# Block-recurrent attention and SwiGLU on one core: pair 5's own weights beside the next batch's scores, small steps on ScalarE, squares summed ahead of the matmul, orders redealt

## The chip, the cores and the metric

The kernel runs on 1 core of one Trainium2 chip. The metric is the time of one execution on the device, in microseconds (us). Times are medians of several executions; the profile is of one further execution, which has its own time. A core has TensorE (PE; its weight loads are shown apart as PEld), VectorE (DVE), ScalarE (ACT), GpSimd (POOL) and SyncE (SP). Each works through its own instructions in the order given; transfers are put on queues, here by SP and by ScalarE.

## The reference

```python
# x (8, 8, 512, 64): batch, head, token, depth; state (8, 8, 32, 64)
scores = scale * np.matmul(x, state.transpose(0, 1, 3, 2))      # scale = 1/8
a = np.exp(scores - scores.max(-1, keepdims=True))
a /= a.sum(-1, keepdims=True) + 1e-09
xread = np.matmul(a, state)                                     # tokens read the states
scores2 = scale * np.matmul(state, x.transpose(0, 1, 3, 2))
a2 = np.exp(scores2 - scores2.max(-1, keepdims=True))
a2 /= a2.sum(-1, keepdims=True) + 1e-09
sread = np.matmul(a2, x)                                        # states read the tokens
x = np.concatenate([xread, sread], axis=2)                      # 544 rows a batch
x = x.transpose(0, 2, 1, 3).reshape(4352, 512)                  # heads side by side
rms = np.sqrt(np.mean(x * x, axis=-1, keepdims=True) + 1e-06)
xn = x / rms * rms_g
g = xn @ w_gate                                                 # 512 -> 1536
silu = g * (1.0 / (1.0 + np.exp(-g)))
return silu * (xn @ w_val) @ w_out                              # 1536 -> 512
```

Everything is float32 to the kernel's matmuls.

## The kernel before

**Tiling.** There are 8 batches of 512 token rows, and at the end the 256 state rows of all batches together. A token's row is its attention weights times the states, so the kernel doesn't form it for the hidden layer: for each batch it multiplies the states with `w_gate` and `w_val` first (the batch's *own weights*), and multiplies the attention weights `aT_s`, already scaled by the norm, with these. The own weights come in six pairs of blocks of 128 hidden columns, pair 0 to pair 5 (`mp`).

**The stages of a batch.** In batches 1 to 7 the hidden layer (`hidden_seven`) takes for each pair seven block products instead of eight (L849; sums of blocks are made beforehand), ScalarE copies them out of PSUM (three copies a pair, L901 among them, and the Silu, L903), VectorE finishes them (L912, L925). The projection (`project_twice`) uses the seven-product scheme at two levels (L1153), with copies by ScalarE (L1166), sums by VectorE and combining steps by GpSimd (`combine`, L1181 and the lines behind it). Batch 0 is computed plainly (L745, L952). The states' rows go through `state_norm`, `hidden_seven` and `project_seven` (L1015).

**The attention of the next batch** runs within the hidden layer and the projection of the present one, in small pieces:

- `scores`: a transpose of the packed state, its copy out of PSUM (L321, `stT`), four VectorE transposes of `x_b` in blocks of 32 (L339), a store of the result to DRAM (`x_d`, L341) and four loads of it in another layout (`xG`, L346), all five on ScalarE's queue; then 8 matmuls of float32 (16 records in the trace) for the scores (L356).
- `tokens_read`: the softmax (exponentials at L428, one for each half `e`), `stT_g`, the states times the norm's weights (L431), the reads (L449), their squares (L456), the row sums (`rms_on_blocks`, with `ss` at L404), the power -0.5 on GpSimd (L300), its spreading along the rows by TensorE (`along_rows`, L307) and the product with `aT_s`.
- `states_read`: a softmax the other way (exponential at L607), the read products (L643), the division by the sum (`sr`, L654), a transpose, and its copy out of PSUM into `xsT` (L660).
- `own_weights`: 8 matmuls (16 records, L702), two copies by ScalarE (L714), four sums by GpSimd (`more_of_v`, L729 and behind). Pairs 0 and 1 are made ahead of their batch, with the projection of the batch before; pairs 2 to 5 within the batch's hidden layer.

The matmuls of the scores, the own weights and the state reads use a part of the PE array each (tiles of 64x32, 128x32; the profile shows the tile's size as 64\*32), and eight or more of them in a row are called a *group* below, as the profile's timeline shows them in one line. Consecutive groups of such tiles, with no 128x128 matmul between, are called a stretch.

**PSUM.** Five pools: `aps` (2 buffers, name `at`), `vps` (2, `pv`), `fx` (2), `fy` and `fz` (1 each, `f`). The scores, the attention's transposes and sums and the own weights of pairs 1, 3 and 5 are in `aps`; those of pairs 0, 2 and 4 in `vps`.

**The order of everything is written out by hand.** Each part of the work is a Python generator, a *stream*; strings of letters say which stream takes its next step: `ORDER` up to batch 0, `FIRST` for batch 1, `PERIOD` for each of batches 2 to 6, `LAST` for batch 7, `STATES` for the end. Every engine's instructions, and the transfers on SP's and ScalarE's queues, come in the order that results. The letters of `PERIOD`:

| letter | stream |
|---|---|
| h, t, u | hidden layer: products (TensorE), copies (ScalarE), sums (VectorE) |
| p, c, k, o | projection: products, copies, sums, stores of the output (SP's queue) |
| v, x | own weights of pairs 2 to 5: products, copies |
| w | `slot_sums`, then the products of pairs 0 and 1 of the next batch |
| a, s | `tokens_read` and `states_read` of the next batch |
| l, f, g | loads of `x` and the state of the batch after next, of the weights, of the quarters' sums, on SP's queue |

In `LAST` the letter a stands for `state_norm` and the sums of the first pair of the states' weights (`sums_of_w`, L806 to L812); in `STATES` y stands for those of the other pairs.

Of the kernel before, what the change touches and what calls it, by code (L numbers as in the profile page):

```python
# [8 lines left out]
F32 = mybir.dt.float32  # L9
# [5 lines left out]
ALU = mybir.AluOpType  # L15
ACTF = mybir.ActivationFunctionType
# [3 lines left out]
P = 128  # L20
# [11 lines left out]
)  # L32

PERIOD = (
    "vlhhatthhtaxxhvuxuthhthuhtauuhhtuhuhuthtahtuaaahuhhtuhuhuxhxtutxhthukkkhtaakavfx"
    "xxvgahuhuthuuuxhthhuuxtahtaaaaahuaxhuthhtuhhthhthhsppusuuuuffutaauuhpsspuppppukp"
    "ukkkkckkaakkgppkkcpppakooskakakakkppppacpppappppcckpfppcakakapppaakkkasskkgkaagg"
    "pppppppppppaakakkooakgapssskaaakkkoosspppcfpaawwsslpssxxxpcoowxxxfg"
)

FIRST = (
    "vqahtaqaahhathhthhqxhuuuxthaqatvquvxthxqxqhtquhuuhhhutqhfqttuaaqxhhhtquqqaaxuhxh"
    "uxhtuthhtvuuhkqktxqhkxukuGhtuaaaahuathhahxtuhGtauhhuuhhutstufhhtusahuuatfuhhpuuu"
    "aphtuuppuplkpfuakkpkppkpkkpppspskcckgkkappkGppkppocapkaggpaakpsokakpppagckpapakk"
    "kskpscakakppkpagkaapagcaappkgaskpkppappkkspsppaposaakkskppppaawcswsxoofsxlpoxwxs"
    "cofxox"
)
LAST = (
    "vxhhffththhtuhhhavuttuuhhtfuhhgxxthhhuuuxxtuthuhtthuhuxhutuvxxxvhthhutkxghhtuhut"
    "kxxhuukhtuhthhthhhhhuuuuttuthhhuuuuhtuhuutuupphuukkppcpapkkkkkpppppppppppkkkpcpp"  # L50
    "ckkppkckpkkpkpckkkpppkkkpkoppkpppagcpppppfkpkkkkkkkkppaaaapkpggppppacpcggooooooo"
    "a"
)
STATES = (
    "hththtyyhuhuhhttuhhhyyytyuhutuhhhutthtuyyhhuuyhhthhhuyututyyyhhtyuhhthuuuhhuhtth"
    "ythuuuyyyutuhuhuytuuyhthhuuhthtuhuhutuuppkhpuucppkkccpkpkpc"
)


# [1 line left out]
def kernel(  # L61
# [23 lines left out]
    B, H, S, D = x.shape  # L85
    Ns = state.shape[2]
# [44 lines left out]
    def load_x(b, *queues):  # L131
# [6 lines left out]
        for c in range(NC):  # L138
# [10 lines left out]

    GE.tensor_tensor(out=consts.tile([P, NC], F32, name="first_pow"), in1=mhalf,  # L150
                     in0=ones.to_broadcast([P, NC]), op=ALU.pow)
    bounds = consts.tile([P, 3], F32, name="bounds")
    for i, bound in enumerate((-896.0 - 7.5 / 16, 1.0, 255.0 * 128)):
        GE.memset(bounds[:, i:i + 1], bound)
    rms_g = consts.tile([P, NI], F32, name="rms_g")

# [156 lines left out]
    def scores(b, packed, soft):  # L313

        xb = x_sb[b]
        stT = one.tile([P, 4, Ns], F32, name="stT")
        tp = aps.tile([P, 4, Ns], F32, name="at")
        TE.transpose(out=tp.rearrange("p j n -> p (j n)"),
                     in_=packed.rearrange("p e d -> p (e d)"), identity=ident)
        yield  # L320
        VE.tensor_copy(stT, tp)  # L321
        yield "step"

        if b < 2:
            xT = one.tile([P, 4, NC, P], F32, name="xT", tag="xT")
            for c in range(NC):
                tp = aps.tile([P, 4, P], F32, name="at")
                for j in range(4):
                    TE.transpose(out=tp[:, j, :], in_=xb[:, c, P * j:P * j + P], identity=ident)  # L329
                yield  # L330
                SE.copy(xT[:, :, c, :], tp)
                yield "step"
            xT = xT.rearrange("p j c t -> p j (c t)")
        else:


            xB = one.tile([P, 4, 4, NC, Ns], F32, name="xB", tag="xT")
            for q in range(4):
                VE.transpose(out=xB[:, q], in_=xb[:, q // 2::2, :, Ns * (q % 2):Ns * (q % 2) + Ns])  # L339
                yield  # L340
            nc.scalar.dma_start(out=x_d[b % 2].rearrange("q g f r -> (g f) q r"),  # L341
                                in_=xB.rearrange("p q j c t -> p q (j c t)"))
            yield
            xT = one.tile([P, 4, 4, P], F32, name="xG", tag="xT")
            for q in range(4):
                nc.scalar.dma_start(  # L346
                    out=xT[Ns * q:Ns * q + Ns].rearrange("f g j r -> f g (j r)"),
                    in_=x_d[b % 2][q].rearrange("g f r -> f g r"))
                yield
            xT = xT.rearrange("p g j r -> p j g r")  # L350


        sp = [aps.tile([P, S], F32, name="at") for e in range(2)]
        for j in range(4):
            for e in range(2):
                TE.matmul(out=sp[e][Ns * j:Ns * j + Ns, :], lhsT=stT[D * e:D * e + D, j, :],  # L356
                          rhs=xT[D * e:D * e + D, j],
                          start=True, stop=True)
        yield


        sS = read[b] = one.tile([P, 2, NC, P], F32, name="sS")
        eS = one.tile([P, 2, S // Ns, Ns], F32, name="eS", tag="eS")
        soft.update(st=stT, e=eS, raw=[eS[:, e] for e in range(2)])
        for e in range(2):
            VE.transpose(out=eS[:, e].rearrange("p k n -> p (k n)"),
                         in_=(sp[e] if b < 2 else
                              sp[e].rearrange("p (g c t) -> p g t c", g=4, c=NC)))
            yield
            SE.copy(sS[:, e].rearrange("p c t -> p (c t)"), sp[e])  # L370
            yield "step" if e else None
# [17 lines left out]
    def rms_on_blocks(b, sq):  # L389


        n = S // Ns
        VE.transpose(out=sq[:, 1, :], in_=sq[:, 0, :])
        yield
        part = one.tile([P, n], F32, name="part")
        VE.reduce_sum(out=part, in_=sq[:, 1, :].rearrange("p (k f) -> p k f", f=Ns), axis=AXX)
        yield
        sp = aps.tile([P, n], F32, name="at")
        TE.matmul(out=sp, lhsT=groups.rearrange("p i t -> p (i t)"), rhs=part,
                  start=True, stop=True)  # L400
        yield
        ss = two.tile([P, NC], F32, name="ss")
        for g in range(4):
            VE.tensor_scalar(ss[Ns * g:Ns * g + Ns], sp[Ns * g:Ns * g + Ns, g::4], 1e-6, None,  # L404
                             op0=ALU.add)
        yield "step"
        ri = mean_root(ss, NC)
        yield
        rp = along_rows(ri, NC)
        yield  # L410
        return rp

    def tokens_read(b):
# [9 lines left out]
        for e in range(2):  # L423
# [4 lines left out]
            SE.activation(out=eS[:, e], in_=eS[:, e], func=ACTF.Exp, scale=SCALE)  # L428
            yield "step"
        stT_g[b] = two.tile([P, 4, Ns], F32, name="stT_g")  # L430
        VE.tensor_tensor(out=stT_g[b], in0=stT, in1=rms_g.unsqueeze(2).to_broadcast([P, 4, Ns]),  # L431
                         op=ALU.mult)
        yield
        aT_s[b] = two.tile([P, 2, S], F32, name="aT_s")
        for e in range(2):
# [153 lines left out]
    def states_read(b):  # L589
# [61 lines left out]
        yield  # L651
        sr = two.tile([P, 2 * D], F32, name="sr")
        for e in range(2):
            VE.tensor_scalar(sr[:, D * e:D * e + D], rp[:, e, :], z2[:, e:e + 1], None,  # L654
                             op0=ALU.mult)
        yield
        tp = aps.tile([P, 4, Ns], F32, name="at")
        TE.transpose(out=tp.rearrange("p j n -> p (j n)"), in_=sr, identity=ident)
        yield
        VE.tensor_copy(xsT[:, :, Ns * b:Ns * b + Ns], tp)  # L660
        yield "step"

    def state_norm():

        sq = one.tile([P, NI, NT], F32, name="sqT", tag="eS")
        SE.activation(out=sq, in_=xsT, func=ACTF.Square, scale=DM ** -0.5)
        yield
        sp = aps.tile([P, NT // P], F32, name="at")
        for r in range(NT // P):
            for i in range(NI):  # L670
                TE.matmul(out=sp[:, r:r + 1], lhsT=sq[:, i, P * r:P * r + P], rhs=ones,
                          start=(i == 0), stop=(i == NI - 1))
        yield
        ss = two.tile([P, NT // P], F32, name="sst")
        VE.tensor_scalar(ss, sp, 1e-6, None, op0=ALU.add)
        ri = mean_root(ss, NT // P)
        yield
        rp = along_rows(ri, NT // P)
        yield
        for i in range(NI):  # L680
            VE.scalar_tensor_tensor(out=xsT[:, i, :], in0=xsT[:, i, :], scalar=rms_g[:, i:i + 1],
                                    in1=rp[:, 0:NT], op0=ALU.mult, op1=ALU.mult)
        sums_of_x()
        yield
# [4 lines left out]
    def own_weights(b, mp):  # L689
# [4 lines left out]
        def products():  # L694
            w = w_sb.pop(b * (NM // 2) + mp)
            for e in range(2):
                pv.append(vps.tile([P, 4 * P], F32, name="pv") if b and mp % 2 == 0 else
                          aps.tile([P, 4 * P], F32, name="at") if b or mp else
                          fx.tile([P, 4 * P], F32, name="f"))
            for j in range(4):  # L700
                for e in range(2):
                    TE.matmul(out=pv[e][Ns * j:Ns * j + Ns, :],  # L702
                              lhsT=stT_g[b][D * e:D * e + D, j, :],
                              rhs=w[D * e:D * e + D, j].rearrange("p m k f -> p (m k f)"),
                              start=True, stop=True)
            if b == 0 or b == 1 and mp < 2:
                fetch(b * (NM // 2) + mp + W_BUFS)
            yield
# [686 lines left out]
```

## Time and profile before

| | us |
|---|---|
| median of 3 runs | 752.94 (752.94, 752.58, 754.74) |
| the profiled execution, its own time | 752.98 |
| its span, first to last instruction | 751.2 |

The mean granted clock of TensorE was 0.999 of full speed. Four periods of the order `PERIOD`, each window from one matmul of the hidden layer to the same matmul of the next batch: the columns are the window, and then the busy time and number of instructions of each engine, the granted clock, the DMA share and GB/s.

| window (us) | length | PE | PEld | DVE | ACT | POOL | clock | DMA share | GB/s |
|---|---|---|---|---|---|---|---|---|---|
| 219.35 to 299.51 | 80.16 | 80.16 | 68.21 | 64.96 | 35.14 | 35.10 | 1.00 | 0.56 | 190 |
| 299.51 to 379.86 | 80.35 | 80.35 | 68.38 | 64.63 | 35.13 | 34.80 | 1.00 | 0.58 | 197 |
| 379.86 to 460.53 | 80.67 | 80.67 | 68.38 | 65.11 | 35.13 | 35.65 | 1.00 | 0.58 | 196 |
| 460.53 to 540.69 | 80.16 | 80.16 | 68.22 | 64.53 | 35.14 | 34.77 | 1.00 | 0.58 | 197 |

Lines of a timeline in the next sections begin with the start and the length of a group of like instructions in us, then the engine, the line, the operation, output <- inputs by the program's names, the tile or shape, and how many instructions it groups. As matmuls overlap, a group's length reaches beyond the start of the next. A line of costliest groups has, behind the shapes and the count, the busy time and the mean ns of one instruction.

### The profile page before, as it was taken

What the parts mean: (1) busy time and instruction counts of PE and PEld (TensorE: products, weight loads), DVE (VectorE), ACT (ScalarE), POOL (GpSimd) and SP (SyncE); (2) the same over time, 40 slices, a digit from 0 to 9 for tenths busy, and PEclk for the clock granted to TensorE, in tenths of its full rate; (3) what the DMA queues carried; (4) which work ended last, traced back from release to release, by engine and by line L of the source; (5) the groups of instructions that cost most, each with busy time, mean ns of one, the idle gap of its engine ahead of it and who ended that gap; (6) DMA issues with size and microseconds to landing.
All of it is one profiled execution on the core that took longest, in us unless ns stands there. A gap on an engine that the chain in (4) does not pass through costs nothing.

```text
span 751.2 us, 14331 instructions
## 1 busy us (share of the span) xinstructions
PE 744.2 (99%) x5636; PEld 598.3 (80%) x5636; DVE 589.4 (78%) x1010; ACT 352.9 (47%) x549; POOL 265.8 (35%) x359
## 2 busy tenths in 40 slices
PE   9999999999999999999999999999999999999997
PEld 7734444779977997889887987799788987899996
DVE  4898968799947995799768994799479955888862
ACT  6999961555155434552265325542555336411220
POOL 3100021531293128432654237503831285224600
PEclk9999999999999999999999999999999999999999
DMA  9997934982784276617672578437760856041411
GB/s 295 288 319 251 366 116 179 319 307 108 229 273 140 75 293 219 224 33 298 212 276 57 191 252 285 115 140 257 236 206 28 309 177 252 20 154 65 149 42 29
DMA packets 60995, 146.16 MB, mean 195 GB/s; under 512 B 14848, under 2 KB 31744, under 8 KB 54016
## 3 DMA queue, kind: packets, MB, share of 16 engines
q1 hardware_dynamic: 47808, 125.78, 47.2%
q10 hardware_dynamic: 13120, 19.47, 8.9%
q8 instruction: 45, 0.74, 0.4%
q14 instruction: 22, 0.18, 0.1%
HBM read 116.46 MB, written 28.77 MB: 193 GB/s over the span
## 4 chain that ended last, share of the span: by engine, by line
PE 98%; DVE 1%; issue 0%; POOL 0%; ACT 0%; POOLq 0%
PE f L849 39%; PE f L1153 31%; PE pv L745 6%; PE f L952 6%; PE at L702 3%; PE pv L702 3%; PE f L1015 2%; PE f L1288 2%; PE at L643 1%; PE at L356 1%; PE at L449 1%; PE at L307 0%; PE pv L516 0%; PE at L329 0%; PE at L617 0%; PE at L511 0%
## 5 line engine op out<-in xcount | busy, mean ns | idle before, releaser
L849 PE MATMUL f<-aT_s,v 128*128 128x256 f32 x504 | 119.3, 382 | 0.0
L849 PEld LDWEIGHTS f<-aT_s,v 128*128 128x128 f32 x504 | 94.7, 190 | 23.2 <-issue 9.2
L1181 POOL TENSOR_TENSOR kept<-kept 128x256 f32<-128x256 f32 x28 | 22.7, 811 | 205.8 <-DVE kept L1193 204.6
L1166 ACT COPY kept<-f 128x512 f32<-128x512 f32 (+1 forms) x56 | 29.6, 531 | 136.8 <-PE f L1153 80.1
L849 PE MATMUL f<-aT_t,vs 128*128 128x256 f32 x336 | 87.0, 383 | 0.0
L912 DVE TENSOR_TENSOR g<-g,f 128x512 f32<-128x512 f32 x84 | 57.3, 686 | 36.3 <-PE f L849 25.2
L1153 PE MATMUL f<-w,h 128*128 128x128 f32 x588 | 74.3, 276 | 0.0
L849 PEld LDWEIGHTS f<-aT_t,vs 128*128 128x128 f32 x336 | 62.7, 190 | 14.6 <-POOL vs L729 3.4
L1153 PEld LDWEIGHTS f<-w,h 128*128 128x128 f32 x588 | 69.6, 192 | 4.2 <-issue 4.1
L903 ACT ACTIVATE hb<-g 128x1024 f32<-128x1024 f32 x42 | 44.4, 1057 | 53.3 <-DVE g L912 53.2
L729 POOL TENSOR_TENSOR vs<-v 128x256 f32<-128x256 f32 x42 | 31.4, 747 | 102.9 <-ACT v L714 102.8
L300 POOL TENSOR_TENSOR ri<-ss,mhalf 128x4 f32<-128x4 f32 (+1 forms) x9 | 11.6, 1291 | 100.8 <-DVE ss L381 72.2
L901 ACT COPY g<-f 128x512 f32<-128x512 f32 x42 | 24.6, 585 | 45.2 <-PE f L849 45.2
L745 PE MATMUL pv<-aT_s,v 128*128 128x512 f32 x96 | 44.1, 598 | 0.0
L952 PE MATMUL f<-wo,hb 128*128 128x512 f32 x96 | 43.8, 597 | 0.0
L849 PE MATMUL f<-aT_s,vs 128*128 128x256 f32 x168 | 43.7, 383 | 0.0
L849 PE MATMUL f<-aT_t,v 128*128 128x256 f32 x168 | 43.4, 381 | 0.0
L1153 PE MATMUL f<-wo,hb 128*128 128x128 f32 x336 | 42.3, 275 | 0.0
L1153 PE MATMUL f<-wo,h 128*128 128x128 f32 x336 | 42.2, 275 | 0.0
L925 DVE TENSOR_TENSOR hb<-hb,f 128x512 f32<-128x512 f32 (+1 forms) x48 | 31.0, 646 | 13.3 <-PE f L849 13.3
L1153 PEld LDWEIGHTS f<-wo,hb 128*128 128x128 f32 x336 | 40.4, 192 | 1.2 <-issue 0.8
L925 DVE TENSOR_TENSOR hb<-hb,c 128x512 f32<-128x512 f32 (+1 forms) x48 | 36.2, 754 | 5.9 <-ACT hb L903 5.1
(225 smaller groups left out, 1649.4 us busy)
## 6 DMA issues: line engine op xcount, KB each, us to landing
w_m<-w_d SPq DMA_DIRECT2D x48, 1024.0 KB
w<-t_d SPq DMA_DIRECT2D x49, 576.0 KB
out_dram<-kept SPq DMA_DIRECT2D x28, 256.0 KB
raw<-in_moe_w_val_dram SPq DMA_DIRECT2D x6, 1024.0 KB
raw<-in_moe_w_out_dram SPq DMA_DIRECT2D x6, 1024.0 KB
w_d<-w_m SPq DMA_DIRECT2D x6, 1024.0 KB
x_b<-in_x_dram SPq DMA_DIRECT2D x6, 1024.0 KB
x_d<-xB ACTq DMA_DIRECT2D x6, 1024.0 KB
```

The costliest lines, as they stand in the source:

```text
L702: TE.matmul(out=pv[e][Ns * j:Ns * j + Ns, :], lhsT=stT_g[b][D * e:D * e + D, j, :], rhs=w[D * e:D * e + D, j].rearrange("p m k f -> p (m k ...
L729: GE.tensor_tensor(out=vs[:, 0], in0=a21, in1=a22, op=ALU.add)
L745: TE.matmul(out=to[0], lhsT=lhs(i, k), rhs=r, start=(i == 0), stop=(i == len(rhs) - 1))
L849: TE.matmul(out=ps[:, i, 0:half], lhsT=l[:, i, :], rhs=r, start=(start and i == 0 and k == 0), stop=(k == len(lhs) - 1), skip_group_check= ...
L901: SE.copy(gates(q)[1], q["x"][:, :, 0:half])
L903: SE.activation(out=hb[:, 2 * mp:2 * mp + 2, 0:n].rearrange("p m (c t) -> p m c t", c=2), in_=q["g"][:, :, :, 0:half], func=ACTF.Silu if s ...
L912: VE.tensor_tensor(out=to, in0=to, in1=q[ps][:, :, 0:half], op=ALU.add)
L925: VE.tensor_tensor(out=part, in0=part, in1=val, op=ALU.mult)
L952: TE.matmul(out=banks[r], lhsT=hb[:, m, P * r:P * r + P], rhs=wo[:, m, :], start=(m == 0), stop=(m == NM - 1))
L1153: TE.matmul(out=to[half][:, slot, :], lhsT=lhs[:, k, :], rhs=rhs[:, k, :], start=(fresh and n in (0, 4) and k == 0), stop=(k == QM - 1), s ...
L1166: SE.copy(of_half(k, i), banks[name][i])
L1181: GE.tensor_tensor(out=k[:, 4:8:3], in0=k[:, 5:6].to_broadcast([P, 2, QD]), in1=k[:, 4:8:3], op=ALU.add)
```

## The change

1. The four order strings `PERIOD`, `FIRST`, `LAST` and `STATES` are dealt anew; `ORDER` stays. In `PERIOD` the product step of pair 5's own weights now follows directly on the step of the scores' matmuls; in the string before, the two stood apart. `PERIOD` has 307 letters before and 307 after.
2. Pair 5's own weights go to the PSUM pool `vps` in place of `aps` (which the scores use).
3. For batches 2 to 7, five steps of the attention go from VectorE to ScalarE: the copies to `stT` and `xsT`, the addition of 1e-6 (`ss`, four instructions; its constant in a fourth column of `bounds`), `stT_g` (four instructions instead of one) and `sr` (two).
4. In `state_norm`, GpSimd sums the four blocks of squares with two additions; then 2 matmuls with a column of ones in place of 8.

The strings of `PERIOD`, before and after (the other three are left out):

```diff
-    "vlhhatthhtaxxhvuxuthhthuhtauuhhtuhuhuthtahtuaaahuhhtuhuhuxhxtutxhthukkkhtaakavfx"
-    "xxvgahuhuthuuuxhthhuuxtahtaaaaahuaxhuthhtuhhthhthhsppusuuuuffutaauuhpsspuppppukp"
-    "ukkkkckkaakkgppkkcpppakooskakakakkppppacpppappppcckpfppcakakapppaakkkasskkgkaagg"
-    "pppppppppppaakakkooakgapssskaaakkkoosspppcfpaawwsslpssxxxpcoowxxxfg"
+    "vahhthtxthahhhhxuutxuthahaaathatuuhluhhuhtvtvfxutuxhaxhthaghuaxhhxuauutfuxhhukkk"
+    "tthhhthgauvuhtuhhkthtauhaaxaxtauhhuausufufxhutsththhaugauuthuhuughupaptuhsuuupkg"
+    "kpkkpkkapppkcppkkpkppcgpppkkpkaapopkspaaapkpkkpppasacpkaaccksppkpkkpcaakspkpaaak"
+    "asaappskpksspskppkaakppkgoooppppkaakappppkasoalwfswossxpxfxcwxxxcoo"
```

The rest of the diff:

```diff
...
@@ -149,8 +149,8 @@
 
     GE.tensor_tensor(out=consts.tile([P, NC], F32, name="first_pow"), in1=mhalf,
                      in0=ones.to_broadcast([P, NC]), op=ALU.pow)
-    bounds = consts.tile([P, 3], F32, name="bounds")
-    for i, bound in enumerate((-896.0 - 7.5 / 16, 1.0, 255.0 * 128)):
+    bounds = consts.tile([P, 4], F32, name="bounds")
+    for i, bound in enumerate((-896.0 - 7.5 / 16, 1.0, 255.0 * 128, 1e-6)):
         GE.memset(bounds[:, i:i + 1], bound)
     rms_g = consts.tile([P, NI], F32, name="rms_g")
 
@@ -318,7 +318,7 @@
         TE.transpose(out=tp.rearrange("p j n -> p (j n)"),
                      in_=packed.rearrange("p e d -> p (e d)"), identity=ident)
         yield
-        VE.tensor_copy(stT, tp)
+        (VE.tensor_copy if b < 2 else SE.copy)(stT, tp)
         yield "step"
 
         if b < 2:
@@ -401,8 +401,8 @@
         yield
         ss = two.tile([P, NC], F32, name="ss")
         for g in range(4):
-            VE.tensor_scalar(ss[Ns * g:Ns * g + Ns], sp[Ns * g:Ns * g + Ns, g::4], 1e-6, None,
-                             op0=ALU.add)
+            SE.activation(out=ss[Ns * g:Ns * g + Ns], in_=sp[Ns * g:Ns * g + Ns, g::4],
+                          func=ACTF.Identity, bias=bounds[Ns * g:Ns * g + Ns, 3:4])
         yield "step"
         ri = mean_root(ss, NC)
         yield
@@ -428,8 +428,13 @@
             SE.activation(out=eS[:, e], in_=eS[:, e], func=ACTF.Exp, scale=SCALE)
             yield "step"
         stT_g[b] = two.tile([P, 4, Ns], F32, name="stT_g")
-        VE.tensor_tensor(out=stT_g[b], in0=stT, in1=rms_g.unsqueeze(2).to_broadcast([P, 4, Ns]),
-                         op=ALU.mult)
+        if b < 2:
+            VE.tensor_tensor(out=stT_g[b], in0=stT,
+                             in1=rms_g.unsqueeze(2).to_broadcast([P, 4, Ns]), op=ALU.mult)
+        else:
+            for j in range(4):
+                SE.activation(out=stT_g[b][:, j], in_=stT[:, j], func=ACTF.Copy,
+                              scale=rms_g[:, j:j + 1])
         yield
         aT_s[b] = two.tile([P, 2, S], F32, name="aT_s")
         for e in range(2):
@@ -651,13 +656,16 @@
         yield
         sr = two.tile([P, 2 * D], F32, name="sr")
         for e in range(2):
-            VE.tensor_scalar(sr[:, D * e:D * e + D], rp[:, e, :], z2[:, e:e + 1], None,
-                             op0=ALU.mult)
+            to, z = sr[:, D * e:D * e + D], z2[:, e:e + 1]
+            if b < 2:
+                VE.tensor_scalar(to, rp[:, e, :], z, None, op0=ALU.mult)
+            else:
+                SE.activation(out=to, in_=rp[:, e, :], func=ACTF.Copy, scale=z)
         yield
         tp = aps.tile([P, 4, Ns], F32, name="at")
         TE.transpose(out=tp.rearrange("p j n -> p (j n)"), in_=sr, identity=ident)
         yield
-        VE.tensor_copy(xsT[:, :, Ns * b:Ns * b + Ns], tp)
+        (VE.tensor_copy if b < 2 else SE.copy)(xsT[:, :, Ns * b:Ns * b + Ns], tp)
         yield "step"
 
     def state_norm():
@@ -665,11 +673,13 @@
         sq = one.tile([P, NI, NT], F32, name="sqT", tag="eS")
         SE.activation(out=sq, in_=xsT, func=ACTF.Square, scale=DM ** -0.5)
         yield
+        for n in (2, 1):
+            GE.tensor_tensor(out=sq[:, 0:n], in0=sq[:, 0:n], in1=sq[:, n:2 * n], op=ALU.add)
+        yield
         sp = aps.tile([P, NT // P], F32, name="at")
         for r in range(NT // P):
-            for i in range(NI):
-                TE.matmul(out=sp[:, r:r + 1], lhsT=sq[:, i, P * r:P * r + P], rhs=ones,
-                          start=(i == 0), stop=(i == NI - 1))
+            TE.matmul(out=sp[:, r:r + 1], lhsT=sq[:, 0, P * r:P * r + P], rhs=ones,
+                      start=True, stop=True)
         yield
         ss = two.tile([P, NT // P], F32, name="sst")
         VE.tensor_scalar(ss, sp, 1e-6, None, op0=ALU.add)
@@ -694,7 +704,7 @@
         def products():
             w = w_sb.pop(b * (NM // 2) + mp)
             for e in range(2):
-                pv.append(vps.tile([P, 4 * P], F32, name="pv") if b and mp % 2 == 0 else
+                pv.append(vps.tile([P, 4 * P], F32, name="pv") if b and mp in (0, 2, 4, 5) else
                           aps.tile([P, 4 * P], F32, name="at") if b or mp else
                           fx.tile([P, 4 * P], F32, name="f"))
             for j in range(4):
```

More of the change, by code (lines that the diff above doesn't have):

```diff
@@ L34 @@
 PERIOD = (
-    "vlhhatthhtaxxhvuxuthhthuhtauuhhtuhuhuthtahtuaaahuhhtuhuhuxhxtutxhthukkkhtaakavfx"
-    "xxvgahuhuthuuuxhthhuuxtahtaaaaahuaxhuthhtuhhthhthhsppusuuuuffutaauuhpsspuppppukp"
-    "ukkkkckkaakkgppkkcpppakooskakakakkppppacpppappppcckpfppcakakapppaakkkasskkgkaagg"
-    "pppppppppppaakakkooakgapssskaaakkkoosspppcfpaawwsslpssxxxpcoowxxxfg"
+    "vahhthtxthahhhhxuutxuthahaaathatuuhluhhuhtvtvfxutuxhaxhthaghuaxhhxuauutfuxhhukkk"
+    "tthhhthgauvuhtuhhkthtauhaaxaxtauhhuausufufxhutsththhaugauuthuhuughupaptuhsuuupkg"
+    "kpkkpkkapppkcppkkpkppcgpppkkpkaapopkspaaapkpkkpppasacpkaaccksppkpkkpcaakspkpaaak"
+    "asaappskpksspskppkaakppkgoooppppkaakappppkasoalwfswossxpxfxcwxxxcoo"
 )
 FIRST = (
[L42 to L46, printed above, removed]
+    "vqahhxtatahqtahahhauhhxuqattuvtqhqquhhthuqhxquuhxhuxhtataquhauxthhthhhququattvtq"
+    "aququqahxahfaaatqahxuuxhuGhhhttuahvhtxakhuaxuhusGGgtushauhxuthuhtaaktguufhhftuhu"
+    "ushukppuhptppapuucgukklpupkkkpkkppkpkkkakapcppkpkaaapapppcppkfckspkaakksaasppppp"
+    "kkpcgpckksppakakakpapkposppakopkpapspskkapoggapkppkpskakaaposwsswwoppxxxxlgxxsfc"
+    "ocfoso"
 )
 LAST = (
[L49 to L52, printed above, removed]
+    "vhhtfthhthxuhguxhtvvhutuhxfhtuthuhhuhhxtuthfxhtuxtxuhxhuhuvtauhhhthxuuthkxthuhhh"
+    "kuututxhxtkhuhhthuuuuhututhhhutuhhutguuthukpuphuuukpppkpkgpckpkppkkakppkppkppkpc"
+    "pkakpppkpkckpkkkpakpcppkkacpopppppppakcokkpkpkkkgppkappapkggkakpppppcfopkopgcooo"
+    "ao"
 )
 STATES = (
-    "hththtyyhuhuhhttuhhhyyytyuhutuhhhutthtuyyhhuuyhhthhhuyututyyyhhtyuhhthuuuhhuhtth"
-    "ythuuuyyyutuhuhuytuuyhthhuuhthtuhuhutuuppkhpuucppkkccpkpkpc"
+    "yyyhhtthhhtuhhuhtuytuythhuhthhuyuhhutyutthhyhhtuyuhuuhththtyyhythyuhuyhuyuuyhhtt"
+    "uhhthuhuutuuythhtuuhhyyhtuphtuuyhuhutuuupcphkcupucppkkpkpkc"
 )
```

## The prediction

> **What bounds the kernel now.** First I read the shares by engine and the granted clock on the page, then the chain that ended last, then the waits of TensorE.
>
> ```profile
> PE 744.2 (99%) x5636; PEld 598.3 (80%) x5636; DVE 589.4 (78%) x1010; ACT 352.9 (47%) x549; POOL 265.8 (35%) x359
> PEclk9999999999999999999999999999999999999999
> PE 98%; DVE 1%; issue 0%; POOL 0%; ACT 0%; POOLq 0%
> PE f L849 <- DVE hb L925: 0.5, 1, 0.5
> ```
>
> TensorE is busy all the time at full clock, it is 98% of the chain, and after the start it waits once, for 0.5 us. Busy alone can hide stalls, so I looked in TensorE's order of time at how far apart the starts are (a float32 matmul shows as two records):
>
> ```profile
> 297.53 1.03 PE L849 MATMUL f<-aT_s,v 128*128 128x256 f32 x4
> 298.49 1.09 PE L702 MATMUL at<-w_m,stT_g 64*32 64x512 f32 x16
> 299.51 2.00 PE L849 MATMUL f<-aT_s,v 128*128 128x256 f32 x8
> 301.34 1.03 PE L849 MATMUL f<-aT_t,vs 128*128 128x256 f32 x4
> 302.20 1.03 PE L849 MATMUL f<-aT_t,v 128*128 128x256 f32 x4
> ...
> 315.15 1.03 PE L849 MATMUL f<-aT_t,vs 128*128 128x256 f32 x4
> 316.11 1.09 PE L702 MATMUL pv<-w_m,stT_g 64*32 64x512 f32 x16
> 316.99 1.06 PE L702 MATMUL at<-w_m,stT_g 64*32 64x512 f32 x16
> 317.99 1.13 PE L849 MATMUL f<-aT_s,vs 128*128 128x256 f32 x4
> ...
> 323.37 1.27 PE L356 MATMUL at<-xG,stT 64*32 64x512 f32 x16
> ...
> 403.71 1.60 PE L356 MATMUL at<-xG,stT 64*32 64x512 f32 x16
> ...
> 658.32 1.84 PE L671 MATMUL at<-ones,sqT 128*128 128x1 f32 x16
> 660.03 1.58 PE L1153 MATMUL f<-wo,h 128*128 128x128 f32 x12
> ```
>
> Undisturbed, four records of 256 columns take 301.34 to 302.20, 0.863 us (0.216 each). Around a stretch of array tiles (64*32) they take longer: 297.53 to 298.49 is 0.957 (0.094 lost going in), and the eight from 299.51 to 301.34 take 1.831 for 1.727 (0.104 lost coming out). A lone group costs 0.094 + 1.019 + 0.104 = 1.217 us; the two groups side by side from 316.11 to 317.99 cost, read in the same way, 0.093 + 1.878 + 0.104 = 2.075. Joining two lone groups therefore saves 2 x 1.217 - 2.075 = 0.359 us. The scores (L356) are such a group, but two of the six that read xG last 1.27 and 1.60 us in place of 1.09: a wait of 0.18 and 0.51 for xG within the group.
>
> **Parts with a price on TensorE.** Both programs were read in their order on each engine. Pieces of tiled work are equal in number; stretches fall from 50 to 45. In batches 2 to 6 the old order has six (a lone own-weights group; a pair; lone scores; the reads; an own-weights group with the state reads; a pair), the new five (pair; scores with pair 5's own weights; reads; state reads with own weights; pair). 5 x 0.359 = 1.79 us. In the first batch and the last the count stays.
>
> state_norm: 16 records from 658.32 to 660.03, 0.112 us apart inside; 12 go: 12 x 0.112 = 1.34 us. [...] The row decides: a one-column matmul here still brings 128x128 weights (192 ns of load each), and starts every 112 ns.
>
> The sum on TensorE is 3.13 us.
>
> **Parts hidden by other work.** The two GpSimd adds: the nearest row is 128x256 in 0.73 us (L1183), so 0.73 + about 1.45 = 2.2 us. The new order ends the norm (its last x_t difference) 11 us of TensorE work ahead of the first state product; uncovered it would cost the 2.2 us.
>
> The five steps on ScalarE are 12 instructions a batch (1 + 4 + 4 + 2 + 1). VectorE loses 0.29 + 0.28 + 4 x 0.16 + 2 x 0.28 + 0.29 = 2.1 us. ScalarE has no such row: bounds are 0.10 us each (0.20 for 128x1, L1313, less the 0.10 by which back-to-back copies overlap) and 0.35 (0.26 for 64x128, L481, plus 0.09, what a bias operand adds: L607 0.718 against L428 0.630). I take 0.2: 2.4 us a batch, into 45 idle us of 80. Two of them stand in short chains. L399 to L307 has 2.8 us of TensorE work between; 0.3 to the first step, 4 x 0.2, and 1.39 for GpSimd's power (L300) make 2.5, so 0.3 remain (0.35 each would overdraw it by 0.3 a batch). State reads to the transpose of sr: 1.15 us of TensorE cover for 0.3 + 2 x 0.25, 0.35 left.
>
> **Queues.** In the new order the four VectorE transposes of x_b stand together and x_d's store leaves ScalarE's queue 17.3 us of TensorE work ahead of the scores, where it was 13.4. Before:
>
> ```profile
> 316.28 1.28 ACTq L346 DMA_DIRECT2D xG<-x_d  x3
> 317.70 0.34 ACTq L346 DMA_DIRECT2D xG<-x_d  x1
> ```
>
> The store was issued at 309.85 and landed 4.3 us later (the trace's semaphore events), so the reads waited for their place on the queue; the last landed 5.7 us after its issue, at 323.41: that is the wait at 323.37. With x_d some 4 us earlier against the scores, the last xG, behind two copies of v, is issued about 6.9 us ahead of them and has some 1.2 us to spare: the 0.18 + 0.51 should go. In the first batch the scores come 5.5 us earlier and x_d only 3; there the last read took 5.8 us, and I charge 0.3.
>
> SP's queue: x_b's load now stands behind two output stores, the second of which waits for GpSimd's four combining steps (2.76 us behind the power). I place its issue 1 us behind the state reads, 9.4 us ahead of the transposes; the load took 8.6 to 9.3 us. VectorE's sums queue behind a late one. Charged nothing; each us late costs up to 1 a batch.
>
> The state FFN's wait (0.5, L925) sits behind two VectorE sums (L806, L808) of 1.48 and 1.37 us beside GpSimd's L1119; the same sums took 0.68 and 0.69 ahead of it. The new order puts seven of them ahead of the first state product, the old one two; I take 0.3 of it.
>
> **Table loads.** The new order has 30 against 20: in batches 2 to 6 the exponential of e = 0 comes ahead of the last Silu, so each gets two more.
>
> ```profile
> 335.30 1.28 ACT L428 ACT_TABLE_LOAD   x1
> 336.59 0.63 ACT L428 ACTIVATE eS<-eS 128x512 f32<-128x512 f32 x1
> ```
>
> The load fills 1.28 us, with no idle time on either side. Counted from the copies ahead of it, copy of z, load (1.28), exponential (0.63), second copy of x (0.59) end some 0.15 us ahead of the matmul that waits for that copy. The Silu's own load falls into the 1.4 us in which it waits for VectorE, and after it L925, which frees the bank for the projection, ends level with its matmul (before: 0.03 to spare). I charge 0.05 a batch, 0.3 in all; bounds 0 and 0.5 a batch (2.5).
>
> **The sum.** -3.13 - 0.69 - 0.3 + 0.3 + 0.3 = -3.5 us. Against the profiled execution: 751.2 - 3.5 = 747.7 of span. It took 752.98 in all, so 1.8 lie around the span, and its time is that of the median, 752.94: 749.4.
>
> **Rivals.** *Tight waits eat it.* Where the new order leaves 0 to 0.3 us (both copies of x, the power, x_b), lateness of 0.5 us in five batches takes back 2.5, and more where two add up: about 752. For it: four such margins in each batch. Against: the old order has margins as small, and waits 1.1 us in all.
>
> *ScalarE's queue becomes the bound (slower).* Place: the stretch from the merged group to the second exponential, where v's copies, scores' copies, two copies of x, and loads stand in one queue and TensorE waits for two of them. If a load in there costs c more than its 1.28, TensorE loses c - 0.15 at the copy and about c - 0.1 behind the Silu: five batches, 5 x (2c - 0.25). From c = 0.5 nothing is left, from 0.7 the kernel is slower; at a second 1.28 it is 749.4 + 11.6 = 761.0. Against it the rows: no gap around any load. [...]
>
> *Joining does not pay,* because scores and own weights have other operands than the pairs seen: only state_norm and the waits remain, 1.34 + 0.4, so 751.2. Against: groups with state reads, another tile shape, join at the same cost.
>
> **How the numbers follow.** Forecast 0.76, tight waits 0.11, ScalarE 0.10, no join 0.03. The forecast's own range goes from all waits gone and nothing new (752.94 - 3.13 - 1.15 = 748.7) to 751; with the tight waits I give 748.5 to 752.2. Less than 0.3% (2.26 us) cannot be told from no change here; faster means under 750.7, slower over 755.2. Faster 0.76, same 0.13 (tight waits, no join, 0.01 of them beyond), slower 0.11.
>
> **What would show it.** TensorE's busy time near 741 us and still 98% of the chain; periods of 80.16 to 80.67 us falling to about 79.8; L356 followed at once by L712 with 1.88 us for both; L681 with 4 records; no L356 over 1.1 us. Wrong it would be if TensorE waits for L911, L935 or L307 in every batch, or if loads show gaps.

## The result, and the profile after

The changed kernel took 776.63 us (median of 4 runs, 772.85 to 778.64) against 753.33 us before: a ratio of 1.0301 (95% interval 1.0255 to 1.0347). It is 3% slower. The profiled execution took 772.85 us with a span of 770.7, 19.5 longer than the span before.

The page of the changed kernel, shares by engine and the chain that ended last; then the waits of TensorE (in total, times, longest):

```profile
PE 747.5 (97%) x5624; PEld 600.3 (78%) x5624; DVE 576.8 (75%) x956; ACT 380.4 (49%) x631; POOL 257.9 (33%) x362
...
PE 58%; DVE 20%; POOL 11%; issue 5%; ACT 3%; DMA 2%; DVEq 0%; ACTq 0%; POOLq 0%
```

```profile
PE f L859 <- ACT g L906: 16.9, 6, 3.5
```

TensorE's part of the chain fell from 98% to 58%, and it now waits six times, at the start of each of the batches 2 to 7, for the copy L906 (L896 before): the first of ScalarE's three copies of a pair of hidden blocks, here that of pair 1. Its busy time is 3.3 us *longer* (747.5 against 744.2), although 12 records are gone. The windows of the five periods, each from the first product of the hidden layer to that of the next batch, show why (length, then busy time by engine, the granted clock, the DMA share and GB/s):

```profile
213.82:296.73 82.91, 80.22 (x664) 68.35 (x664) 62.77 (x106) 39.60 (x71) 31.79 (x44) 1.00 0.57 191
296.73:381.72 84.99, 81.93 (x663) 69.48 (x663) 62.99 (x106) 40.19 (x73) 33.31 (x46) 0.98 0.57 186
381.72:466.70 84.98, 81.91 (x663) 69.44 (x663) 62.98 (x106) 40.19 (x73) 33.30 (x46) 0.98 0.57 186
466.70:550.02 83.32, 80.25 (x663) 68.30 (x663) 62.51 (x106) 40.20 (x73) 33.30 (x46) 1.00 0.58 190
550.02:635.07 85.05, 81.57 (x663) 69.22 (x662) 62.97 (x106) 40.03 (x73) 33.12 (x46) 0.98 0.56 185
```

Every period has some 3 us without work for TensorE (82.91 less 80.22). In three of them TensorE is also busy 1.3 to 1.7 us longer, and there its mean clock is 0.98. Now the third of the six waits, at the start of batch 4, on TensorE, ScalarE, GpSimd and SP's queue, from the timeline:

```profile
388.83 1.03 PE L859 MATMUL f<-aT_t,v 128*128 128x256 f32 x4
392.92 1.13 PE L859 MATMUL f<-aT_t,vs 128*128 128x256 f32 x4 [3.07 <-ACT g L906]
393.89 1.72 PE L859 MATMUL f<-aT_s,vs 128*128 128x256 f32 x4
395.41 2.92 PE L859 MATMUL f<-aT_s,v 128*128 128x256 f32 x8
```

```profile
387.25 1.06 ACT L913 ACTIVATE hb<-g 128x1024 f32<-128x1024 f32 x1
392.28 0.59 ACT L906 COPY g<-f 128x512 f32<-128x512 f32 x1 [3.97 <-DMA out_dram<-kept]
```

```profile
383.62 0.73 POOL L742 TENSOR_TENSOR vs<-v,vs 128x256 f32<-128x256 f32 x1
384.31 0.73 POOL L739 TENSOR_TENSOR vs<-v 128x256 f32<-128x256 f32 x1
...
387.18 0.73 POOL L1191 TENSOR_TENSOR kept<-kept 128x256 f32<-128x256 f32 x1
...
389.21 0.72 POOL L1196 TENSOR_TENSOR kept<-kept 128x256 f32<-128x256 f32 x1
```

```profile
379.01 0.42 SPq L134 DMA_DIRECT2D x_b<-in_x_dram  x1
379.52 1.92 SPq L196 DMA_DIRECT2D w_m<-w_d  x2
389.96 0.39 SPq L1274 DMA_DIRECT2D out_dram<-kept  x1
```

Read from the end back: TensorE stands until 392.92 for L906. L906 waits 3.97 us for the *store* of the last output block of the batch before, called c21 in the kernel: c21 and the copies of the hidden pairs take turns in the two buffers of the tag `g`, and pair 1's copy gets the one that c21 has just left. The store is issued at 389.96, when GpSimd's combining step ends (L1191 to L1196); and that step waited in GpSimd's queue behind the sums of pair 0 *and* pair 1 (L739 to L742, four each). In the kernel before it stood between the two. There SP's queue had one load of weights and that of x ahead of the store; in the new order it is two of weights and that of x:

```profile
375.46 0.73 POOL L732 TENSOR_TENSOR vs<-v,vs 128x256 f32<-128x256 f32 x1
376.15 0.73 POOL L1181 TENSOR_TENSOR kept<-kept 128x256 f32<-128x256 f32 x1
...
378.86 0.73 POOL L729 TENSOR_TENSOR vs<-v 128x256 f32<-128x256 f32 x1
```

```profile
370.83 0.49 SPq L196 DMA_DIRECT2D w_m<-w_d  x1
371.41 0.41 SPq L134 DMA_DIRECT2D x_b<-in_x_dram  x1
378.92 0.39 SPq L1264 DMA_DIRECT2D out_dram<-kept  x1
```

In the fence of TensorE, the four matmul records from 393.89 and the eight from 395.41 take longer than the 1.03 and 1.89 us that such groups take elsewhere: the granted clock was 0.5 from 394.07 to 397.49.

**The sum of the 19.5 us.** Gaps between starts of TensorE's records, beyond the steady spacing, at the six places: 2.86 + 3.22 + 3.23 + 3.24 + 3.65 + 1.72 = 17.9. Three stretches of 3.41 us at half clock: 1.6 + 1.7 + 1.6 = 4.9. The rest is 19.5 - 22.8 = -3.3 us. The prediction's sum was -3.5.

### The profile page after: what moved, and what is told of

Read it like the earlier page. It is cut to its first block, busy times and chain, and to the rows that moved or that the text cites. A ratio compares the mean times of both kernels' runs of the same rounds, so it can differ in the third digit from the quotient of the medians.

```text
span 770.7 us, 14302 instructions
## 1 busy us (share of the span) xinstructions
PE 747.5 (97%) x5624; PEld 600.3 (78%) x5624; DVE 576.8 (75%) x956; ACT 380.4 (49%) x631; POOL 257.9 (33%) x362
## 4 chain that ended last, share of the span: by engine, by line
PE 58%; DVE 20%; POOL 11%; issue 5%; ACT 3%; DMA 2%; DVEq 0%; ACTq 0%; POOLq 0%
PE f L859 27%; PE f L1163 9%; PE pv L755 5%; PE f L962 5%; DVE hb L1222 2%; PE f L1025 2%; PE f L1298 2%; PE pv L712 2%; DMA out_dram<-kept 2%; PE at L712 2%; POOL kept L1193 2%; DVE g L922 2%; DVE h L1217 2%; POOL kept L1191 1%; POOL kept L1196 1%
## 5 line engine op out<-in xcount | busy, mean ns | idle before, releaser
L859 PEld LDWEIGHTS f<-aT_s,v 128*128 128x128 f32 x504 | 96.4, 194 | 19.2 <-DVE h L1217 4.2
L1191 POOL TENSOR_TENSOR kept<-kept 128x256 f32<-128x256 f32 x28 | 20.8, 744 | 195.8 <-DVE kept L1203 126.9
L739 POOL TENSOR_TENSOR vs<-v 128x256 f32<-128x256 f32 x42 | 30.8, 734 | 144.9 <-ACT v L724 144.8
L935 DVE TENSOR_TENSOR hb<-hb,f 128x512 f32<-128x512 f32 (+1 forms) x48 | 31.2, 650 | 28.1 <-PE f L859 28.0
L859 PE MATMUL f<-aT_s,vs 128*128 128x256 f32 x168 | 45.6, 396 | 0.0
L300 POOL TENSOR_TENSOR ri<-ss,mhalf 128x4 f32<-128x4 f32 (+1 forms) x9 | 9.4, 1049 | 105.1 <-DVE ss L381 72.2
L906 ACT COPY g<-f 128x512 f32<-128x512 f32 x42 | 24.5, 583 | 39.3 <-DMA out_dram<-kept 24.2
L1163 PEld LDWEIGHTS f<-wo,h 128*128 128x128 f32 x336 | 39.9, 192 | 0.0
```

The costliest lines, as they stand in the source:

```text
L739: GE.tensor_tensor(out=vs[:, 0], in0=a21, in1=a22, op=ALU.add)
L859: TE.matmul(out=ps[:, i, 0:half], lhsT=l[:, i, :], rhs=r, start=(start and i == 0 and k == 0), stop=(k == len(lhs) - 1), skip_group_check= ...
L906: SE.copy(gates(q)[0], q["x"][:, :, 0:half])
L935: VE.tensor_tensor(out=part, in0=part, in1=val, op=ALU.mult)
L1163: TE.matmul(out=to[half][:, slot, :], lhsT=lhs[:, k, :], rhs=rhs[:, k, :], start=(fresh and n in (0, 4) and k == 0), stop=(k == QM - 1), s ...
L1191: GE.tensor_tensor(out=k[:, 4:8:3], in0=k[:, 5:6].to_broadcast([P, 2, QD]), in1=k[:, 4:8:3], op=ALU.add)
```

## The experiments

Three theories. A: the store of c21 is *issued* too late (the combining step behind pair 1's sums). B: the store *lands* late, because two loads of weights (1 MB each, one more than before) and the load of x stand ahead of it on SP's queue. C: ScalarE's order (the small steps, the table loads) is what costs, and the wait is only where it shows.

**The combining step earlier.** The letter c ahead of pair 1's last x, which is the step that issues the four sums (in `FIRST` alike):

```diff
-    "...wossxpxfxcwxxxcoo"
+    "...wossxpxfxcwxxcxoo"
```

> The changed kernel with one letter moved: the last combining step on GpSimd (the c21 step) stands ahead of pair 1's four sums instead of behind them, in batches 1 to 6. TensorE's, VectorE's and ScalarE's orders stay as they are. Theory A (the store of c21 is issued too late, and pair 1's first copy on ScalarE waits for its buffer): four sums take 2.9 us, so the store is issued 2.9 us earlier, TensorE's waits of 2.9 to 3.65 us at six places shrink to about 0.3 each, no stretch at half clock is left within the kernel, and the time is 749.5 + 6 x 0.3 = about 751. Theory B (the store lands late because the transfers ahead of it on SP's queue hold it up): the store is issued earlier but lands at the same moment, about 770. Theory C (ScalarE's order, with the small steps and the two more table loads a batch, is what costs): ScalarE's order is untouched, so at least 760.

Measured: 774.78 us, ratio 1.0298 (1.0268 to 1.0328). A alone falls; it is near what B said, and within what C said (at least 760). ScalarE's and SP's lines at the same place:

```profile
391.52 1.06 ACT L913 ACTIVATE hb<-g 128x1024 f32<-128x1024 f32 x1
396.43 0.59 ACT L906 COPY g<-f 128x512 f32<-128x512 f32 x1 [3.85 <-DMA out_dram<-kept]
```

```profile
383.79 1.93 SPq L196 DMA_DIRECT2D w_m<-w_d  x2
391.38 0.39 SPq L1274 DMA_DIRECT2D out_dram<-kept  x1
```

The store is issued 2.9 us earlier, measured from pair 0's copy, but it takes 5 us to land instead of 2.2, and so lands at the same moment (table below). So the late step alone does not explain the wait.

**Another buffer.** All orders as they are; c21 uses the buffer `eS`, idle at that time, in batches 1 to 6:

```diff
-    k = kept[what] = (two if pool == "g" else seven["k"]).tile(
-        [P, 8, QD], F32, name="kept", tag="g" if pool == "g" else "kept")
+    own = what == "c21" and b < B - 1
+    k = kept[what] = (one if own else two if pool == "g" else seven["k"]).tile(
+        [P, 8, QD], F32, name="kept",
+        tag="eS" if own else "g" if pool == "g" else "kept")
```

> The changed kernel, all orders as they are; in batches 1 to 6 the c21 result gets the attention's idle buffer eS instead of the tag g, which pair 1's copies use next. Theory A: the copy of pair 1 waits for nothing, no wait of TensorE is left, and the time is that of the prediction's sum, about 749.4. Theory B: the store lands as late as before the edit, but nobody waits for it: 749 to 750 too. Theory C: at least 760.

Measured: 751.67 us, ratio 0.9981 (0.9972 to 0.999). Its one wait of TensorE after the start, and the sum over the five periods:

```profile
PE at L318 <- ACT v L724: 0.2, 1, 0.2
```

```profile
sum 399.90, PE 399.69 PEld 341.82 DVE 313.82 ACT 199.90 POOL 164.89; mean PE 79.94 PEld 68.36 DVE 62.77 ACT 39.98 POOL 32.98
```

The waits are gone, and the granted clock is 1.0 from 7.3 to 748.0 us: the reuse of this one buffer was the whole loss, and C falls (ScalarE's work is the same as in the changed kernel). A and B are not told apart by this run.

**The late step in the kernel before.** Batches 2 to 6, nothing else:

```diff
-    "...slpssxxxpcoowxxxfg"
+    "...slpssxxxpwxxxcoofg"
```

> The kernel before, with nothing of the change but this: in batches 2 to 6 the last combining step (c21) stands behind pair 1's four sums on GpSimd. Theory A: the store is issued about 2.9 us later, pair 1's first copy starts about 3.1 us later than it did, of which TensorE has 0.7 to spare; five waits of about 2.4 us, 12 us: about 765, and a few us more where a window falls under the clock's threshold. Theories B and C (transfers ahead on the queue; ScalarE's steps): within 1 us of the kernel before, 753.

Measured: 762.79 us, ratio 1.0128 (1.0113 to 1.0143). A is enough by itself: five waits for L896, 7.9 us, longest 1.7 (expected 2.4 each), and no stretch at half clock.

**The loads later.** `fetch_late` moves the two f of `...alwfswossxpxfxcw...` behind the last o; `fix_both` does this and the earlier combining step; `fix_one` does the earlier step and moves only the second f (`FIRST` alike):

```diff
-    "...alwfswossxpxfxcwxxxcoo"
+    "...alwswossxpxxcwxxxcooff"    fetch_late
+    "...alwswossxpxxcwxxcxooff"    fix_both
+    "...alwfswossxpxxcwxxcxoof"    fix_one
```

> The changed kernel with two loads of weights (1 MB each) moved on SP's queue from ahead of the last output store (c21) to behind it, in batches 1 to 6; the combining step stays behind pair 1's sums. Two causes, each enough (theory AB: the step on GpSimd makes the store's issue late, 7.1 us after pair 0's first copy, and the loads ahead hold back its landing to 9.3 us after that copy even where it is issued at 4.3, as the run with the earlier combining step showed): the store is still issued at 7.1, lands some 2.2 us later, and TensorE still waits about 3.2 us six times: 772 to 778. Theory B alone (only the loads ahead matter): the waits go, 750 to 752.

> Both moves together: the combining step ahead of pair 1's four sums, and the two loads of weights behind the last store. Theory AB: the store is issued 4.3 us after pair 0's first copy, lands 2.2 to 2.5 us later at about 6.6; pair 1's copy starts at 6.9 where TensorE would need it at 6.2: waits of 0.3 to 0.7 us at five or six places, no stretch at half clock: 2 to 4 us above the run with the other buffer (751.67), so 753 to 756. If something else on the queue holds the store (x_b's load of 1 MB, the quarters' sums), waits of 2 us and more stay, over 762.

> The changed kernel with the combining step ahead of pair 1's four sums, and one of the two loads of weights (1 MB, not 2) behind the last store, in batches 1 to 6. Theory AB: the store is issued 4.3 us after pair 0's first copy with 1 MB less ahead of it; at the 350 GB/s or so of that stretch this is 2.9 us, so it lands at 9.3 - 2.9 = 6.4 to 6.6 and TensorE waits 0.4 to 1.0 us at that place. With both loads behind the store, three loads stood in a row, the store of x_d on ScalarE's queue was slowed and a second wait came up behind it (1.3 to 2.3 us a batch, about 10 in the last): with one load behind, this second wait should be under 1 us a batch and gone in the last: 753 to 760. If it is the order of the loads as such that collides with x_d, as before: 768 to 774.

Measured: 789.4 us (ratio 1.0493, 1.0473 to 1.0514), 772.46 (1.0268, 1.0249 to 1.0287) and 764.02 (1.0132, 1.0104 to 1.016). In all three the first wait goes roughly as was said; each missed the time, for a second reason. The start of batch 4, in us after pair 0's first copy (from the starts and semaphore events of the trace), and the gap on TensorE:

| run | step ends | store issued | store landed | pair 1's copy starts | gap |
|---|---|---|---|---|---|
| before | 3.55 | 3.57 | 6.02 | 6.67 | 0 |
| changed | 7.10 | 7.13 | 9.35 | 9.45 | 3.23 |
| step earlier | 4.25 | 4.28 | 9.23 | 9.33 | 3.19 |
| loads later | 7.10 | 7.13 | 9.87 | 9.97 | 3.73 |
| both | 4.15 | 4.17 | 6.92 | 7.03 | 0.91 |
| step, one load | 4.22 | 4.25 | 7.39 | 7.49 | 1.37 |
| other buffer | 6.86 | 6.89 | 9.10 | 5.39 | 0 |
| late step in before | 6.41 | 6.44 | 9.18 | 9.28 | 1.84 |

There are two causes, and in the new order each is enough for the whole wait: only with both mended does the store land ahead of 7. Even then a gap of 0.91 is left, because the new order also wants pair 1's copy sooner: with the other buffer it starts at 5.39, where it was 6.67 before. And the moved loads are missed elsewhere. In `fix_both`, on ScalarE's queue in batch 3, and TensorE's waits:

```profile
315.65 0.31 ACTq L346 DMA_DIRECT2D xG<-x_d  x1
316.00 0.58 ACT L911 COPY g<-f 128x512 f32<-128x512 f32 x1 [3.88 <-DMA x_d<-xB]
```

```profile
PE f L859 <- ACT g L911: 6.2, 5, 2.1
PE at L712 <- DMA w_m<-w_d: 5.7, 1, 5.7
...
PE f L859 <- ACT g L906: 1.6, 3, 0.7
```

Three loads of 1 MB now follow each other, and in batch 3 the store of x_d takes 11.6 us to land, against 5.3 in the run with the other buffer; the load of xG waits for it on ScalarE's queue, and the copy L911 waits behind that load. That the loads slow the store is read from the order on the queues and these times; no run shows it by itself. In the last batch the own weights (L712) wait for their load, 9.1 us in `fetch_late`, 5.7 in `fix_both`, 4.5 in `fix_one`, each followed by half clock. So the loads stood early for a reason, and of the orders that were tried none mends the wait without opening another; the buffer does.

**A longer wait.** The third combining addition done five times in batches 1 to 6, to see what the length of the wait does to the clock:

```diff
-    GE.tensor_tensor(out=k[:, 7], in0=k[:, 2], in1=k[:, 1], op=ALU.add)
+    for _ in range(5 if what == "c21" and b < B - 1 else 1):
+        GE.tensor_tensor(out=k[:, 7], in0=k[:, 2], in1=k[:, 1], op=ALU.add)
```

> The changed kernel with the third combining addition of c21 done five times in batches 1 to 6 (four times too often, about 0.45 us each), which delays the store by 1.8 us more. Theory A: each of the six waits of TensorE grows by 1.8 us, to 3.5 to 5.5: 11 us. Theory on the clock: windows of 3.41 us whose activity is under about a third are followed by one at half clock, which costs about 1.7 us; at waits of 5 us each of the last five or six is followed by one, in place of three in the profiled run: 772.85 + 10.9 + 2 or 3 x 1.7 = 787 to 789 against a run with three. If the half clock came by chance and not by the length of the wait, about three again: 784. Theory C: under 776 (GpSimd's work does not matter).

Measured: 797.1 us (ratio 1.0592, 1.0567 to 1.0616), 8 above what was expected. The five additions took 3.03 us where the one took 0.46, so the store was delayed by 2.6 and not 1.8, and the six waits came to 31.0 us in place of 17.9. Five of the six are followed by half clock, as the theory had it, but for 6.83 us each and not 3.41. Its "about a third" is what the changed kernel's windows show: with an activity (3.41 us less the idle time, as a share) of 0.34 or less half clock followed, with 0.43 or more it did not. Over the seven runs with waits the border lies between 0.39 and 0.43 (last section).

**The parts of the sum.** First part 4 of the change alone in the kernel before (`state_norm`, with both additions just ahead of the matmuls), then (`rest_alone`) the run with the other buffer without part 4:

```diff
+        for n in (2, 1):
+            GE.tensor_tensor(out=sq[:, 0:n], in0=sq[:, 0:n], in1=sq[:, n:2 * n], op=ALU.add)
         sp = aps.tile([P, NT // P], F32, name="at")
```

> The kernel before with the change's state_norm alone (two additions on GpSimd, 2 matmuls instead of 8). By the row, 12 records of 0.112 us go: 1.34 us less, about 751.6, and 4 records of that line in the trace. [...] If the two additions are not covered: up to 2.4 us more.

> The run with the other buffer, and state_norm as in the kernel before (8 matmuls, no additions on GpSimd): all of the change but that part, without the wait on the store. By the profile of the run with the other buffer, its five periods were 1.6 us shorter than the kernel before's, batch 1 was 0.36 longer and the first hidden product of the states did not wait (0.5): 751.2 of the kernel before's 753 (1.5 to 2 us less). If the redealt order and the joins are worth nothing in sum, and the whole of what the other buffer's run gained was state_norm: 753, no difference.

Measured: 751.14 us against 753.25 (0.9974, 0.9964 to 0.9984), and 751.32 against 753.51 (0.9972, 0.9959 to 0.9985). In the second one wait came that the run with the other buffer did not have: 1.1 us at the start of batch 1, again for L906 (here L905), which stood 3.2 us for the store of batch 0's last output (`ot`, in the tag `g` too). The run with the earlier combining step had it also (1.2 us); the buffer of c21 does not cure this place. In the first run the last batch, from its first hidden product to that of the states, shrank by 1.34 us in the trace (74.68 to 73.34), the term of the prediction to the digit. TensorE's records there:

```profile
658.30 0.50 PE L672 MATMUL at<-ones,sqT 128*128 128x1 f32 x4
658.67 1.58 PE L1154 MATMUL f<-wo,h 128*128 128x128 f32 x12
```

Then the join undone, and the five steps back on VectorE, both on the run with the other buffer:

```diff
-    "tthhhthgauvuhtuhh..."
+    "tthhhthgauuhvtuhh..."
```

```diff
-        (VE.tensor_copy if b < 2 else SE.copy)(stT, tp)
+        VE.tensor_copy(stT, tp)
...
```

> The run with the other buffer (751.67, periods of 79.94 to 80.25 us), and pair 5's own weights one product of the hidden layer later than the scores, so that the two groups stand apart again in batches 2 to 6. If joining two groups is worth 0.359 us: periods 0.36 longer, 1.8 us in all, about 753.4. If joining is worth nothing for these operands: periods the same.

> The run with the other buffer, and the five small steps back on VectorE, every other order as it is. If the steps on ScalarE are worth nothing on TensorE's path (the prediction charged and credited nothing but the small margins): periods within 0.2 us of 79.94 to 80.25 and a time of 751 to 752.5. If VectorE's 2.1 us a batch were what made room, periods up to 2 us longer, 761; if the chain over ScalarE costs (the power, the transpose of sr), periods shorter by up to 0.3.

Measured: 752.88 us (0.9998, 0.9988 to 1.0009) and 754.04 (1.0021, 1.0008 to 1.0033). The five periods without the join:

```profile
sum 401.63, PE 401.43 PEld 340.79 DVE 314.41 ACT 199.56 POOL 164.73; mean PE 80.28 PEld 68.16 DVE 62.88 ACT 39.91 POOL 32.95
```

401.63 - 399.90 = 1.73 us for five joins, 0.346 each (the prediction had 0.359). And with the steps on VectorE, a wait of 0.7 us in every period:

```profile
PE f L1163 <- DVE h L1215: 3.3, 5, 0.9
```

The projection waits for VectorE's half sums: in this order the move to ScalarE is worth about 0.7 us a batch (403.46 against 399.90 over the five periods), which lies between the sides of the expectation (nothing, or up to 2 us).

## Why the prediction was wrong

The forecast, 749.4, failed by 27 us, and its sign with it, on one step: the part on queues. It followed x_b, x_d and xG along SP's and ScalarE's queues, wrote "Charged nothing" behind SP's, and did not follow the last output store: what it waits for, what stands ahead of it, and who waits for its buffer. The charge of nothing was the term that failed: the runs showed 17.9 us of waits there, and 4.9 us of half clock behind three of them, of which the prediction had no term at all. Its signs of being wrong named the copy L911 and the sum L935, never the copy L906. None of its rivals had this mechanism; the one on ScalarE's queue named another place and another cause, and the run with the other buffer, where the same table loads cost TensorE nothing, refutes it.

Most of the wait could have been worked out. In the profile before, the combining step ends 3.55 us after pair 0's copy. The new order puts four sums ahead of it, 2.87 in all: 6.4. A store takes 2.45 more (table): 8.9. Pair 1's copy is wanted sooner than before, since a lone group of own weights (1.217) no longer stands between: 6.67 - 1.22 = 5.45, and the product behind it had 0.8 to spare (the copy ends at 222.09, the product starts at 222.91 in batch 2). 8.9 - 5.45 - 0.8: by this estimate some 2.6 us a batch, 16 in six. The trace had 17.9; the step ended at 7.1, as pair 0's copy itself starts 0.7 earlier against GpSimd's sums. The half clock could not be had from that profile, in which TensorE never stands for more than 0.5 us after the start.

**The rest of the sum** held by the stages of the trace, less well by the medians. By stages, the run with the other buffer against before: batch 1 +0.36 (charged 0.3); periods 401.50 to 399.90, -1.60; last batch -1.28 (1.34); states up to their last matmul -0.67 (the wait of 0.5 went, of which 0.3 had been taken). That is -3.2. A start that came 1.0 us later and 0.3 behind the last matmul leave -1.9 of span in that execution. The periods were -1.6 where joins (1.73) and the two waits for xG (0.69) make 2.4: so 0.8 went to small new costs, 0.16 a batch against 0.05 charged. One of them shows, the 0.2 us at L318. No score group lasts over 1.09 us, TensorE is busy for 742.2 us (near 741 was foretold), and L681 has its 4 records. Gaps on ScalarE's loads: none, as the row had it (0.02 us ahead of each of the 30); the small ScalarE steps took 0.21 us (`stT_g`, `sr`) and 0.27 (`ss`) from start to start, where 0.2 was taken. Joining saved nearly what the prediction took from its rows (0.346 us each against 0.359), so its rival that joining does not pay falls too.

What stays open: the medians give the run with the other buffer 0.1% to 0.28% less than before, 0.8 to 2.1 us, below the 3.2 of the stages; and the medians of its two halves alone, each about 2 us faster, do not add up in it. In the traces they do: from the first hidden product to the last matmul, `norm_alone` is 1.6 us shorter than the kernel before and `rest_alone` 0.6, or 1.7 without its wait of 1.1. The first hidden product came anywhere from 133.2 to 134.4 us in these runs, whatever the kernel, so up to 1 us of start lies in each figure; whether that is the whole of the difference is not shown.

## What to carry to other kernels

When an order is dealt anew, check each buffer that goes round at a stage's edge: who reads it last (a store counts until it has landed: L906 stood 3.97 us for one), what stands ahead of that reader on *each* queue, and when the next writer comes; a writer that comes earlier is as dangerous as a reader that goes later. Where a wait has two causes that are each enough, mending one shows nothing, so an experiment that takes the dependence itself away (a buffer) comes first. The stalls of TensorE cost more than their length here: 4.9 us of half clock came on top of 17.9 us of waits (next section).

## What the runs showed of the hardware

TensorE's clock went to half for whole windows of 3.41 us. In the changed kernel these begin on one grid: at 308.74, 394.07 and 561.33 us, 25 and 49 windows of 3.413 apart. What decided was the idle time inside one such window: over seven runs with waits, each window at full clock with 2.09 us of idle time or more (19 of them) was followed by half clock, and none with 1.93 or less was (the changed kernel's own windows lay on both sides: 2.26, 2.61 and 3.34 against 1.24 to 1.93). The idle time is worked out from the starts of TensorE's records and their steady spacing. So of the changed kernel's waits of 3.22, 3.23 and 3.24 us the first two cost some 1.7 more each and the third nothing, by where they fell on the grid. The changed kernel's times go with that: 772.85 with a mean clock of 0.993, and 775.28 to 778.64 with 0.991 to 0.988; 0.005 of the clock over 776.6 us is 3.9 of the 5.8 us between the extremes. Of the 19 half-clock stretches ten lasted one window: there the wait had ended before the stretch began, or at most 0.30 us into it. Eight lasted two windows and one three: there the wait reached 0.64 us or more into the stretch. The rule behind this stays open.
